# First turn's K and R turned as they come and scaled on the way out of PSUM

## The chip, the cores and the metric

The kernel runs on one core of a Trainium2 chip. A time is the device time of one execution in microseconds (us). Engines are named as in the profile: PE (TensorE matmul), PEld (its weight load), DVE (VectorE), ACT (ScalarE), POOL (GpSimd) and SP (SyncE, which here only issues transfers). A line L353 is a line of the kernel file before the change, unless the text says otherwise.

## The reference, cut to what matters

An RWKV-5 recurrence over 4 batches, 8 heads, 768 steps and head size 48 feeds a router with 8 experts:

```python
for t in range(S):
    cur = einsum('bhd,bhe->bhde', u * k_t, v_t)
    y[:, :, t] = einsum('bhd,bhde->bhe', r_t, state + cur)
    state = w * state + einsum('bhd,bhe->bhde', k_t, v_t)
x = y.transpose(0, 2, 1, 3).reshape(B * S, H * D)      # 3072 rows of 384
logits = normalized(x) @ normalized(expert_emb).T / tau
out[rows of e] = gate * relu(x @ w1[e]) @ w2[e]         # each row to its best expert
```

The change touches only the beginning of the recurrence.

## The kernel before, in words

The 768 steps are cut into 6 chunks of 128, and each chunk is worked in two turns, each with two of the four batches. So there are 12 turns, numbered t = 0 to 11, and the two batches of a turn are called u = 0 and u = 1. Within a chunk the recurrence becomes matrix products: K and R are scaled by powers of the decay w, the scores are R times K transposed under a mask, and a state of 48x48 per head is carried from chunk to chunk.

The steps of a turn, with the functions that issue them:

- `load`: K, R and V come as one transfer of 192 KB each per batch (128 partitions x 8 heads x 48 words); from turn 4 on each is cut in two. Nearly all are issued by SP, in the order of the code; the two of R in turn 0 by ACT's queue.
- `scale_r`, `scale_k` (L353, L348): R and K, rows being steps, times the tables `rpow` and `kpow`. DVE does it in turn 0, POOL in all later turns. For t > 0 the first of a turn waits for the first half of the previous turn's scores.
- `turn_in` (L369): four PE transposes each bring the scaled tile into PSUM. `take_in` (L374, L376): ACT copies the turned tile to SBUF as `KT` and the first half of `RT`. `own_r` (L382): DVE multiplies the turned R by u times w, the second half of `RT`, which serves the step's own term.
- `scores` (L395): 64 PE products per turn. `mask` and `own_terms` (L410, L417): DVE takes them out under the masks `smask` and `dmask`.
- `outer` (L431): scaled K times V, for the state. `half_state`, `next_state` and `decay_state` (L445 to L458) carry the state on DVE and POOL.
- `with_v` (L486) and `with_state` (L505), a turn later, give y; `turn_y` and `take_x` (L520, L524) turn it back into rows, `keep_x` stores them.

Before the first turn `build_first` makes the tables. DVE waits for `w` (four words per partition, two small transfers), fills a step tile, and a scan (L114) makes the powers; L119 and L121 make the tables `kp` (for K) and `rp` (for R) with channels on partitions. PE transposes them (L128) and DVE copies them to `kpow` and `rpow` (L133), with steps on partitions. Ahead of that, PE runs three products of ones (L99, the constant `WAKE`), and a fourth after the tables. POOL makes the identity and the masks.

The order of all other work is written by hand: `attention` puts every step at a planned time (`plan.at`), and the program emits steps in order of those times. The times set only the order in which each engine's instructions stand; each engine runs its own list in order and waits on semaphores. At turn 1 to 3, loads are emitted as K, K, R, R, V, V, three planned periods (9.4 each) ahead. `load_small` fetches the expert embeddings (`emb`), `tau` and w as one row; `embeddings_a` uses `emb` on ACT (L252) and then on POOL (L253 to L258).

SP's list is in order too. Completion of transfers is counted on eight semaphores in rotation, so a transfer waits until the one eight places before it has landed.

```python
def scale_r(k, t, u):
    q = k.nc.gpsimd if t else k.nc.vector
    ins = q.tensor_mul(of(k.Rw, t)[:, u, :, 0:D], of(k.R, t)[:, u], k.rpow)
    if t and u == 0:
        after(k, ins, k.scored)
```

Of the kernel before, what the change touches and what calls it, by code (L numbers as in the profile page):

```python
# [10 lines left out]
F32 = mybir.dt.float32  # L11
# [64 lines left out]
def build_first(k):  # L76

    nc, pool = k.nc, k.const
    wc = k.wc0 = pool.tile([128, NP], F32, name="wc")
    nc.vector.memset(wc, 1.0)  # L80
    k.ones = pool.tile([128, 128], F32, name="ones")
    nc.vector.memset(k.ones, 1.0)
    wide = scratch(k.YT[2], 0)
    nc.vector.memset(wide, 1.0)
    with nc.allow_non_contiguous_dma(reason="384 words"):
        for s in range(2):
            q = nc.sync if s == 0 else nc.scalar
            q.dma_start(out=wc[s * DP : s * DP + D, :], in_=k.w.rearrange("(p s) d -> s d p", s=2)[s])
    for which in range(3):
        for u in range(2):  # L90
            load(k, 0, which, u, paced=False)
    uw = k.aconst.tile([128, NP], F32, name="uw")
    nc.vector.memset(uw, 0.0)
    with nc.allow_non_contiguous_dma(reason="384 words"):
        for s in range(2):
            nc.scalar.dma_start(out=uw[s * DP : s * DP + D, :], in_=k.u.rearrange("(p s) d -> s d p", s=2)[s])

    def idle(i):
        nc.tensor.matmul(k.bank[(6 + i) % 8], k.ones, wide, start=True, stop=True)  # L99

    for i in range(WAKE):
        idle(i)
    k.ident = pool.tile([128, 128], F32, name="ident")
    make_identity(nc, k.ident)
    step, seed = (k.AT[1][:, i].rearrange("q r (p i) -> q (r p) i", i=C) for i in range(2))
    nc.gpsimd.memset(seed, 0.0)
    nc.gpsimd.memset(seed[:, :, 0:1], 1.0)

    nc.vector.tensor_scalar(wc, wc, W_MIN, W_MAX, ALU.max, ALU.min)
# [11 lines left out]
    nc.vector.tensor_mul(rp, t, over_i)  # L121
    k.kpow = k.aconst.tile([128, H, D], F32, name="kpow")
# [7 lines left out]
    build_masks(k)  # L130
    for src, dst, bank in tables:
        ps = bank.rearrange("q (p s d) -> q p s d", p=NP, s=2)
        nc.vector.tensor_copy(dst.rearrange("q (p s) d -> q p s d", s=2), ps[:, :, :, 0:D])  # L133
    k.tables = t, uw


def tables_u(k):
    k.uw = k.aconst.tile([128, NP], F32, name="uw2")
    k.nc.vector.tensor_mul(k.uw, k.tables[1], k.wc0)


def tables_w(k):
# [13 lines left out]
def build_masks(k):  # L156
    nc, pool = k.nc, k.const
    k.umask = pool.tile([128, 128], F32, name="umask")
    nc.gpsimd.memset(k.umask, 0.0)
    nc.gpsimd.affine_select(  # L160
        out=k.umask, in_=k.umask, compare_op=ALU.is_ge, fill=1.0,
        base=0, pattern=[[-1, 128]], channel_multiplier=1,
    )

    k.smask = k.aconst.tile([128, HC], F32, name="smask")
    k.dmask = k.aconst.tile([128, HC], I32, name="dmask")
    for s in range(2):
        nc.vector.tensor_copy(k.smask[halves(s), :], k.umask[halves(s), halves(s)])
        nc.vector.tensor_copy(k.dmask[halves(s), :], k.ident[halves(s), halves(s)])


def numbers(k, name, shape, pattern, base, step):
# [113 lines left out]
def rings(k):  # L286

    nc, pool = k.nc, k.aconst

    def ring(name, count, shape, pad=None, pool=pool):  # L290
        out = []
        for i in range(count):
            t = pool.tile(shape, F32, name=f"{name}{i}")
            if pad is not None:
                nc.gpsimd.memset(t[:, :, :, D:DP], 0.0)
            out.append(t)
        return out

    k.K = ring("K", 3, [128, 2, H, D], pool=k.long)
    k.R = ring("R", 3, [128, 2, H, D], pool=k.long)  # L300
    k.Rw = ring("Rw", 2, [128, 2, H, DP], True, k.long)
    k.V = ring("V", 4, [128, 2, H, DP])
    k.Kw = ring("Kw", 2, [128, 2, H, DP], True, k.long)
# [25 lines left out]
def load(k, t, which, u, part=slice(0, H), paced=True):  # L329

    c, bp = divmod(t, 2)
    src, ring = ((k.k, k.K), (k.r, k.R), (k.v, k.V))[which]
    q = k.nc.scalar if which == 1 and t == 0 else k.nc.sync
    ins = q.dma_start(
        out=of(ring, t)[:, u, part, 0:D],
        in_=src[2 * bp + u, part, c * C : (c + 1) * C, :].rearrange("h s d -> s h d"),
    )
    if paced:
        after(k, ins, k.last)


def pair(t, p):
# [2 lines left out]

def scale_k(k, t, u):
    q = k.nc.gpsimd if t else k.nc.vector
    q.tensor_mul(of(k.Kw, t)[:, u, :, 0:D], of(k.K, t)[:, u], k.kpow)  # L348


def scale_r(k, t, u):
    q = k.nc.gpsimd if t else k.nc.vector
    ins = q.tensor_mul(of(k.Rw, t)[:, u, :, 0:D], of(k.R, t)[:, u], k.rpow)  # L353
    if t and u == 0:
        after(k, ins, k.scored)


# [6 lines left out]


def turn_in(k, t, u, which):
    src, bank = of(k.Kw if which else k.Rw, t), k.turned[u][which]
# [11 lines left out]


def own_r(k, t, u):
    k.nc.vector.tensor_mul(  # L382
        of(k.RT, t)[:, u, :, :, 1, :], k.turned[u][0].rearrange("q (p s i) -> q p s i", p=NP, s=2),
        k.uw[:, :, None, None].to_broadcast([128, NP, 2, HC]),
    )
# [435 lines left out]
def attention(k):  # L821
# [4 lines left out]
    for t in range(TURNS):  # L826
# [3 lines left out]
        for i in range(6 if t else 0):  # L830
            when = at - 3 * P + 0.5 + 1.55 * i
            if t < 4:
                plan.at(when, load, k, t, i // 2, i % 2, slice(0, H), False)
                continue
            for j in range(2):
                plan.at(when + 0.75 * j, load, k, t, i // 2, i % 2, slice(j * NP, (j + 1) * NP))
        for u in range(2):
            for which in range(2):

                place = which if t else 1 - which  # L840
                plan.at(before + 1.0 + 2 * u + place, scale_k if which else scale_r, k, t, u)
                plan.at(before + 3.3 + 2.35 * u + 0.47 * place, turn_in, k, t, u, which)
                plan.at(before + 3.8 + 2.4 * u + 0.6 * place, take_in, k, t, u, which)
            plan.at(before + (4.0 if t else 5.3) + 2.6 * u, own_r, k, t, u)
# [926 lines left out]
```

## Time and profile before

| what | us |
|---|---|
| median of 3 runs (lowest, highest) | 410.56 (407.46, 411.36) |
| the profiled execution, its whole time | 410.78 |
| its span, first to last instruction | 408.9 |
| PE busy in the span | 386.8 (95%) |
| DVE / ACT / POOL busy | 228.0 / 143.6 / 130.2 |
| scores of turns 0, 1, 2, 3 begin | 11.68, 18.23, 27.56, 38.99 |

The profile gives instructions in order of time with start, duration, engine, line, operation, output and inputs, shape and count; in square brackets stands the idle time of the engine before the instruction and what seems to have ended it. DMA figures are means over the core's 16 DMA engines. A start of "SPq" or "ACTq" is the issue of a transfer by that queue, not its data. The trace also records each transfer's packets and the moments at which its semaphore was raised; where the text says that something landed, it is the last of these.

### The profile page before, as it was taken

What the parts mean: (1) busy time and instruction counts of PE and PEld (TensorE: products, weight loads), DVE (VectorE), ACT (ScalarE), POOL (GpSimd) and SP (SyncE); (2) the same over time, 40 slices, a digit from 0 to 9 for tenths busy, and PEclk for the clock granted to TensorE, in tenths of its full rate; (3) what the DMA queues carried; (4) which work ended last, traced back from release to release, by engine and by line L of the source; (5) the groups of instructions that cost most, each with busy time, mean ns of one, the idle gap of its engine ahead of it and who ended that gap; (6) DMA issues with size and microseconds to landing.
All of it is one profiled execution on the core that took longest, in us unless ns stands there. A gap on an engine that the chain in (4) does not pass through costs nothing.

```text
span 408.9 us, 12450 instructions
## 1 busy us (share of the span) xinstructions
PE 386.8 (95%) x5118; PEld 345.3 (84%) x5118; DVE 228.0 (56%) x582; ACT 143.6 (35%) x367; POOL 130.2 (32%) x167
## 2 busy tenths in 40 slices
PE   7888899899998999899999999999999999999993
PEld 3677788797897899879899999999998989979882
DVE  7866677787788580522852645445454464374331
ACT  1355464546462624221133214313412413413400
POOL 2584656564653231602133013104303412012001
PEclk9999999999999999999999999999999999999998
DMA  9998768877717357734834252514605553001001
GB/s 136 159 163 168 150 146 173 171 160 152 155 44 235 117 175 232 247 124 158 299 117 113 101 184 87 159 43 172 194 25 190 142 185 117 0 19 38 2 19 47
DMA packets 95460, 54.40 MB, mean 133 GB/s; under 512 B 78723, under 2 KB 90034, under 8 KB 95394
## 3 DMA queue, kind: packets, MB, share of 16 engines
q1 hardware_dynamic: 89426, 43.67, 42.1%
q0 software_dynamic: 3264, 9.44, 6.9%
q10 hardware_dynamic: 2704, 0.40, 0.7%
q8 instruction: 42, 0.69, 0.7%
q14 instruction: 24, 0.20, 0.2%
HBM read 44.20 MB, written 9.58 MB: 132 GB/s over the span
## 4 chain that ended last, share of the span: by engine, by line
PE 83%; issue 4%; POOL 2%; DVE 1%; ACT 0%; POOLq 0%; DVEq 0%
PE ps L1131 15%; PE ps L1264 12%; PE pu L1131 8%; PE ps L1044 6%; PE pu L1264 5%; PE ps L395 4%; PE ps L1294 4%; PE ps L369 4%; PE ps L1301 3%; PE py L486 3%; PE pu L1294 3%; PE py L1044 2%; PE pu L431 2%; PE pu L520 2%; PE py L505 2%
## 5 line engine op out<-in xcount | busy, mean ns | idle before, releaser
L1233 POOL DMA_INDIRECT out_dram<-y,goes x27 | 30.8, 1140 | 174.0 <-ACT y L1348 90.9
L1011 POOL DMA_INDIRECT G<-xs,take x23 | 24.3, 1058 | 30.6 <-PE py L1031 8.6
L1131 PE MATMUL ps<-xTe,w 128*128 128x192 f32 (+3 forms) x160 | 31.4, 333 | 0.0
L353 POOL TENSOR_TENSOR Rw<-R,rpow 128x384 f32<-128x384 f32 x22 | 22.8, 1034 | 19.4 <-DMA R<-in_r_dram 10.1
L1044 PE MATMUL ps<-RT,w 128*128 128x128 f32 x204 | 26.6, 279 | 1.4 <-ACT K L1047 0.5
L1131 PEld LDWEIGHTS ps<-xTe,w 128*128 128x128 f32 x160 | 27.5, 190 | 0.0
L1286 DVE SCALAR_TENSOR_TENSOR y<-ps,lists_sorted,kept 128x192 f32<-128x192 f32 x18 | 7.1, 416 | 35.6 <-ACT kept L1278 21.8
L1044 PEld LDWEIGHTS ps<-RT,w 128*128 128x128 f32 x204 | 24.3, 192 | 2.4 <-ACT K L1047 1.0
L1264 PE MATMUL ps<-T,RT 128*128 128x192 f32 x144 | 26.0, 328 | 0.0
L395 PE MATMUL ps<-RT,KT 48*64 48x128 f32 x768 | 25.1, 273 | 0.7 <-DVE RT L382 0.5
L395 PEld LDWEIGHTS ps<-RT,KT 48*64 48x64 f32 x768 | 21.3, 133 | 3.9 <-issue 2.9
L1264 PEld LDWEIGHTS ps<-T,RT 128*128 128x128 f32 x144 | 23.6, 190 | 0.6 <-ACT kept L1278 0.6
L348 POOL TENSOR_TENSOR Kw<-K,kpow 128x384 f32<-128x384 f32 x22 | 23.4, 1066 | 0.0
L376 ACT COPY RT<-ps 128x512 f32<-128x512 f32 x24 | 14.1, 588 | 21.0 <-PE ps L369 16.6
L382 DVE TENSOR_TENSOR RT<-ps,uw 128x512 f32<-128x512 f32 x24 | 16.6, 690 | 8.0 <-ACT RT L376 7.9
L1131 PE MATMUL ps<-Tx,S 128*128 128x192 f32 (+3 forms) x96 | 20.3, 341 | 0.0
L1149 ACT COPY kept<-ps 128x384 f32<-128x384 f32 (+3 forms) x24 | 11.8, 490 | 22.7 <-PE ps L1131 17.5
L1061 DVE TENSOR_TENSOR RT<-ps,kept 128x384 f32<-128x384 f32 (+1 forms) x15 | 8.5, 566 | 19.9 <-PE ps L1131 19.5
L410 DVE TENSOR_TENSOR AT<-ps,smask 128x256 f32<-128x256 f32 x48 | 18.5, 412 | 1.4 <-PE ps L395 1.4
L417 DVE COPY_PREDICATED AT<-dmask,ps 128x256 f32<-128x256 int32 x48 | 18.4, 437 | 0.0
L1101 ACT COPY xTe<-py 128x384 f32<-128x384 f32 (+3 forms) x18 | 8.8, 490 | 27.0 <-PE py L1108 26.9
L1131 PEld LDWEIGHTS ps<-Tx,S 128*128 128x128 f32 x96 | 16.1, 190 | 2.1 <-ACT kept L1149 2.1
(342 smaller groups left out, 885.9 us busy)
## 6 DMA issues: line engine op xcount, KB each, us to landing
w<-in_moe_w_dram SPq DMA_DIRECT2D x24, 512.0 KB
w<-in_moe_w_dram SPq DMA_DIRECT2D x32, 384.0 KB
xs<-X SPq DMA_DIRECT2D x24, 192.0 KB
K<-in_k_dram SPq DMA_DIRECT2D x32, 96.0 KB
R<-in_r_dram SPq DMA_DIRECT2D x32, 96.0 KB
V<-in_v_dram SPq DMA_DIRECT2D x32, 96.0 KB
K<-in_k_dram SPq DMA_DIRECT2D x8, 192.0 KB
V<-in_v_dram SPq DMA_DIRECT2D x8, 192.0 KB
```

The source lines that it names most:

```text
L348: q.tensor_mul(of(k.Kw, t)[:, u, :, 0:D], of(k.K, t)[:, u], k.kpow)
L353: ins = q.tensor_mul(of(k.Rw, t)[:, u, :, 0:D], of(k.R, t)[:, u], k.rpow)
L382: k.nc.vector.tensor_mul(of(k.RT, t)[:, u, :, :, 1, :], k.turned[u][0].rearrange("q (p s i) -> q p s i", p=NP, s=2), k.uw[:, :, None, None ...
L395: ins = k.nc.tensor.matmul(k.D[2 * u + par][halves(s), p * C : (p + 1) * C], KT[rows, u, p, halves(s)], RT[rows, u, p, s].rearrange("q j i ...
L410: k.nc.vector.tensor_mul(of(k.AT, t)[:, u, par].rearrange("q (p i) -> q p i", p=NP), kinds(k, u, par)[:, :, 0], k.smask[:, None, :].to_bro ...
L417: k.nc.vector.copy_predicated(of(k.AT, t)[:, u, par].rearrange("q (p i) -> q p i", p=NP), k.dmask[:, None, :].to_broadcast([128, NP, HC]), ...
L1011: k.nc.gpsimd.indirect_dma_start(out=G[0:n, :], out_offset=None, in_=k.xs[0:rows, :], in_offset=IndirectOffsetOnAxis(ap=(k.take_first if f ...
L1044: k.last = k.nc.tensor.matmul(ps, w1[:, m, f * 128 : (f + 1) * 128], x_of(k, e, m)[:, cols], start=(m == 0), stop=(m == NK - 1))
L1131: k.last = nc.tensor.matmul(ps[:, i * h : (i + 1) * h], a[:, g, i * 128 : (i + 1) * 128], b, start=start and i == 0, stop=True, skip_group ...
L1233: k.nc.gpsimd.indirect_dma_start(out=out[:, :], out_offset=IndirectOffsetOnAxis(ap=k.goes[0:n, e, t : t + 1], axis=0), in_=y[0:n, :], in_o ...
L1264: k.last = nc.tensor.matmul(ps, a(q), b[:, q], start=start and q == 0, stop=True, skip_group_check=True,)
L1294: k.last = nc.tensor.matmul(p.z, h_one(k, e, f)[:, 256:384], w2[:, f, :], start=(f == 0), stop=(f == NF - 1))
```

## The change

Five things change, all in the first turns.

- **Turn 0's K and R are turned raw.** They are loaded into `Kw[1]` and `Rw[1]` (the padded tiles that turn 1's scaled K and R will take later), PE turns them unscaled, ahead of the tables' transposes, and DVE multiplies them by `kp` and `rp` (channels on partitions) as it takes them out of PSUM. ACT's four copies of turn 0 and DVE's two scalings of R go. Turn 0's scaled K by rows, which `outer` needs, is made by DVE after that.
- **R times u in turn 0** is done by ACT from SBUF, in four instructions per batch with u times w as a scale column, in place of one DVE instruction from PSUM.
- **Tables and masks.** The tables' transposes and copies move behind the first K and R; ACT makes the copies to `kpow` and `rpow`, and the copies of `smask`. The fourth product of ones goes. POOL's clearing of the pads of `Kw` and `Rw` moves from the start to behind the masks.
- **Order of transfers.** `u` is fetched right behind `w`, ahead of K and R. Then SP's order is: K of turn 0; K, R, K, R of turn 1; V of turn 0; K, R, K, R of turn 2; V of turn 1; V of turn 2; one K of turn 3; `emb`, `tau`, w's row; the other K of turn 3; R and V of turn 3. Before it was K, V of turn 0; K, R, V of turn 1; `emb`, `tau`, w's row; K, R, V of turn 2; K, R, V of turn 3. From turn 4 on it is as before.
- **One wait goes**: the scaling of turn 1's R on POOL no longer waits for turn 0's scores.

```diff
     with nc.allow_non_contiguous_dma(reason="384 words"):
-        for s in range(2):
-            q = nc.sync if s == 0 else nc.scalar
-            q.dma_start(out=wc[s * DP : s * DP + D, :], in_=k.w.rearrange("(p s) d -> s d p", s=2)[s])
-    for which in range(3):
-        for u in range(2):
+        for dst, src in ((wc, k.w), (uw, k.u)):
+            for s in range(2):
+                q = nc.sync if s == 0 else nc.scalar
+                q.dma_start(out=dst[s * DP : s * DP + D, :], in_=src.rearrange("(p s) d -> s d p", s=2)[s])
+
+    for u in range(2):
+        for which in range(2):
             load(k, 0, which, u, paced=False)
...
+    build_masks(k)
+    for X in (k.Kw[1], k.Rw[1], k.Kw[0], k.Rw[0]):
+        nc.gpsimd.memset(X[:, :, :, D:DP], 0.0)
...
+    nc.vector.tensor_mul(k.uw, uw, wc)
+    k.tables = t, rp, kp
+
+
+def tables_rows(k):
+
     k.kpow = k.aconst.tile([128, H, D], F32, name="kpow")
     k.rpow = k.aconst.tile([128, H, D], F32, name="rpow")
-    tables = ((kp, k.kpow, k.U[0]), (rp, k.rpow, k.U[1]))
-    for src, dst, bank in tables:
+    for src, dst, bank in ((k.tables[2], k.kpow, k.U[0]), (k.tables[1], k.rpow, k.U[1])):
         ps = bank.rearrange("q (p s d) -> q p s d", p=NP, s=2)
         for p in range(NP):
-            nc.tensor.transpose(ps[:, p].rearrange("q s d -> q (s d)"), src[:, p, :], k.ident)
-    idle(WAKE)
...
+            k.nc.tensor.transpose(ps[:, p].rearrange("q s d -> q (s d)"), src[:, p, :], k.ident)
+        k.nc.scalar.copy(dst.rearrange("q (p s) d -> q p s d", s=2), ps[:, :, :, 0:D])
...
+    dst = raw(k, which) if t == 0 and which < 2 else of(ring, t)
...
+def raw(k, which):
+    return (k.Kw[1], k.Rw[1])[which]
...
 def scale_k(k, t, u):
     q = k.nc.gpsimd if t else k.nc.vector
-    q.tensor_mul(of(k.Kw, t)[:, u, :, 0:D], of(k.K, t)[:, u], k.kpow)
+    q.tensor_mul(of(k.Kw, t)[:, u, :, 0:D], of(k.K, t)[:, u] if t else raw(k, 0)[:, u, :, 0:D], k.kpow)
 
 
 def scale_r(k, t, u):
-    q = k.nc.gpsimd if t else k.nc.vector
-    ins = q.tensor_mul(of(k.Rw, t)[:, u, :, 0:D], of(k.R, t)[:, u], k.rpow)
-    if t and u == 0:
+    ins = k.nc.gpsimd.tensor_mul(of(k.Rw, t)[:, u, :, 0:D], of(k.R, t)[:, u], k.rpow)
+    if t > 1 and u == 0:
         after(k, ins, k.scored)
...
 def take_in(k, t, u, which):
-    if which:
+    if t == 0:
+        src = k.turned[u][which].rearrange("q (p i) -> q p i", p=NP)
+        if which:
+            k.nc.vector.tensor_mul(of(k.KT, t)[:, u], src, k.tables[2])
+        else:
+            k.nc.vector.tensor_mul(
+                of(k.RT, t)[:, u, :, :, 0, :], src.rearrange("q p (s i) -> q p s i", s=2),
+                k.tables[1].rearrange("q p (s i) -> q p s i", s=2),
+            )
+    elif which:
...
 def own_r(k, t, u):
+    if t == 0:
+        for p in range(NP):
+            R = of(k.RT, t)[:, u, p]
+            k.nc.scalar.mul(R[:, :, 1, :], R[:, :, 0, :], k.uw[:, p : p + 1])
+        return
...
             if t < 4:
-                plan.at(when, load, k, t, i // 2, i % 2, slice(0, H), False)
+
+                if t < 3 and i > 3:
+                    continue
+                plan.at(when, load, k, t, i // 2 if t > 2 else i % 2, i % 2 if t > 2 else i // 2, slice(0, H), False)
+                if t < 3 and i == 3:
+                    for v in ((0,), (1, 2))[t - 1]:
+                        for w in range(2):
+                            plan.at(when + 0.1 * v + 0.01, load, k, v, 2, w, slice(0, H), False)
                 continue
...
-    plan.at(-P + 0.4, load_small, k)
-    plan.at(-P + 5.25, tables_u, k)
+    plan.at(0.6, load_small, k)
+    plan.at(-P + 3.95, tables_rows, k)
+    for u in range(2):
+        plan.at(0.05 + 0.01 * u, scale_k, k, 0, u)
```

More of the change, by code (lines that the diff above doesn't have):

```diff
@@ L80, in build_first @@
     nc.vector.memset(wc, 1.0)
+    uw = k.aconst.tile([128, NP], F32, name="uw")
+    nc.vector.memset(uw, 0.0)
     k.ones = pool.tile([128, 128], F32, name="ones")
@@ L85, in build_first @@
     with nc.allow_non_contiguous_dma(reason="384 words"):
-        for s in range(2):
-            q = nc.sync if s == 0 else nc.scalar
-            q.dma_start(out=wc[s * DP : s * DP + D, :], in_=k.w.rearrange("(p s) d -> s d p", s=2)[s])
-    for which in range(3):
-        for u in range(2):
-            load(k, 0, which, u, paced=False)
[L92 to L96, printed above, removed]
+        for dst, src in ((wc, k.w), (uw, k.u)):
[4 more added lines that the diff above has]
+        for which in range(2):
+            load(k, 0, which, u, paced=False)
     def idle(i):
@@ L121, in build_first @@
     nc.vector.tensor_mul(rp, t, over_i)
+    k.uw = k.aconst.tile([128, NP], F32, name="uw2")
+    nc.vector.tensor_mul(k.uw, uw, wc)
+    k.tables = t, rp, kp
+def tables_rows(k):
     k.kpow = k.aconst.tile([128, H, D], F32, name="kpow")
     k.rpow = k.aconst.tile([128, H, D], F32, name="rpow")
-    tables = ((kp, k.kpow, k.U[0]), (rp, k.rpow, k.U[1]))
-    for src, dst, bank in tables:
+    for src, dst, bank in ((k.tables[2], k.kpow, k.U[0]), (k.tables[1], k.rpow, k.U[1])):
         ps = bank.rearrange("q (p s d) -> q p s d", p=NP, s=2)
         for p in range(NP):
-            nc.tensor.transpose(ps[:, p].rearrange("q s d -> q (s d)"), src[:, p, :], k.ident)
-    idle(WAKE)
[L130 to L139, printed above, removed]
+            k.nc.tensor.transpose(ps[:, p].rearrange("q s d -> q (s d)"), src[:, p, :], k.ident)
+        k.nc.scalar.copy(dst.rearrange("q (p s) d -> q p s d", s=2), ps[:, :, :, 0:D])
 def tables_w(k):
@@ L167, in build_masks @@
     for s in range(2):
-        nc.vector.tensor_copy(k.smask[halves(s), :], k.umask[halves(s), halves(s)])
         nc.vector.tensor_copy(k.dmask[halves(s), :], k.ident[halves(s), halves(s)])
+        nc.scalar.copy(k.smask[halves(s), :], k.umask[halves(s), halves(s)])
 def numbers(k, name, shape, pattern, base, step):
@@ L300, in rings @@
     k.R = ring("R", 3, [128, 2, H, D], pool=k.long)
-    k.Rw = ring("Rw", 2, [128, 2, H, DP], True, k.long)
+    k.Rw = ring("Rw", 2, [128, 2, H, DP], None, k.long)
     k.V = ring("V", 4, [128, 2, H, DP])
-    k.Kw = ring("Kw", 2, [128, 2, H, DP], True, k.long)
+    k.Kw = ring("Kw", 2, [128, 2, H, DP], None, k.long)
     k.RT = ring("RT", 3, [128, 2, NP, 2, 2, HC], pool=k.long)
@@ L333, in load @@
     q = k.nc.scalar if which == 1 and t == 0 else k.nc.sync
+    dst = raw(k, which) if t == 0 and which < 2 else of(ring, t)
     ins = q.dma_start(
-        out=of(ring, t)[:, u, part, 0:D],
+        out=dst[:, u, part, 0:D],
         in_=src[2 * bp + u, part, c * C : (c + 1) * C, :].rearrange("h s d -> s h d"),
@@ L366, in turn_in @@
 def turn_in(k, t, u, which):
-    src, bank = of(k.Kw if which else k.Rw, t), k.turned[u][which]
+    src, bank = of(k.Kw if which else k.Rw, t) if t else raw(k, 1 - which), k.turned[u][which]
     for p in range(NP):
@@ L840, in attention @@
                 place = which if t else 1 - which
-                plan.at(before + 1.0 + 2 * u + place, scale_k if which else scale_r, k, t, u)
+                if t:
+                    plan.at(before + 1.0 + 2 * u + place, scale_k if which else scale_r, k, t, u)
                 plan.at(before + 3.3 + 2.35 * u + 0.47 * place, turn_in, k, t, u, which)
                 plan.at(before + 3.8 + 2.4 * u + 0.6 * place, take_in, k, t, u, which)
-            plan.at(before + (4.0 if t else 5.3) + 2.6 * u, own_r, k, t, u)
+            plan.at(before + (4.0 if t else 4.75) + 2.6 * u, own_r, k, t, u)
             plan.at(at + 0.9 * u, scores, k, t, u)
```

## The prediction, made before the changed kernel was run

> **What bounds the kernel now.** I read the chain that ended last first: PE holds 83% of it, and its traced part begins only at 35.61 us. The change touches turns 0 to 2, that is the first 30 us, so what counts is when each later turn's work may begin on PE, and what that waits for. That is read from the timeline of 0 to 30 us, of every engine:
>
> ```profile
> 3.18 0.29 DVE L109 TENSOR_SCALAR wc<-wc 128x4 f32<-128x4 f32 x1 [1.59 <-DMA wc<-in_w_dram]
> ...
> 7.48 1.02 PE L99 MATMUL ps<-YT,ones 128*128 128x512 f32 x2
> ...
> 11.68 2.08 PE L395 MATMUL ps<-RT,KT 48*64 48x128 f32 x64 [0.48 <-DVE RT L382]
> ...
> 13.52 1.00 POOL L353 TENSOR_TENSOR Rw<-R,rpow 128x384 f32<-128x384 f32 x1 [10.08 <-DMA R<-in_r_dram]
> ...
> 18.23 2.23 PE L395 MATMUL ps<-RT,KT 48*64 48x128 f32 x64
> ...
> 21.06 1.00 POOL L353 TENSOR_TENSOR Rw<-R,rpow 128x384 f32<-128x384 f32 x1 [1.60 <-PE py L486]
> ...
> 27.56 2.09 PE L395 MATMUL ps<-RT,KT 48*64 48x128 f32 x61
> ...
> 29.45 0.20 POOL L258 MEMSET ent<- 128x128 f32 x1
> ...
> 29.62 1.00 POOL L353 TENSOR_TENSOR Rw<-R,rpow 128x384 f32<-128x384 f32 x1
> ```
>
> The scores (L395) of turns 0, 1, 2 begin at 11.68, 18.23, 27.56. Turn 0 hangs on a chain of small steps from `w`. Turns 1 to 3 begin with POOL's scaling of R, and there the trace's landing records (when a transfer's semaphore reached its count) say what releases it: R of turn 1 landed at 13.35 (POOL 13.52), of turn 2 at 20.93 (POOL 21.06, though the view names PE), of turn 3 at 29.39 (POOL 29.62). All three are transfers. The third is the one that matters most below.
>
> The windows of one us, columns PE busy, granted clock, DMA share, GB/s, show that the input stream runs without pause except three times:
>
> ```profile
> 17.00:18.00 1.00, 1.00 (x27) 1.00 1.02 156
> 18.00:19.00 1.00, 1.00 (x31) 1.00 0.11 19
> ...
> 24.00:25.00 1.00, 0.84 (x56) 1.00 0.45 56
> ...
> 28.00:29.00 1.00, 1.00 (x43) 1.00 0.33 67
> ```
>
> Each dip follows, by about 2.3 us, a 16 KB instruction packet (packet records: 16.06, 21.92, 25.95 us, each holding one DMA engine for 1.1 to 1.7 us), while one SP issue takes 2.1 to 2.7 us instead of about 1 (R at 15.61, K at 21.89, V at 26.07). So up to 29 us the loads are a queue of 192 KB pieces, about 1.04 us each, and a piece lands by its place in that queue.
>
> **Part by part: turn 0.** `w` stays first in both queues, so DVE's chain from 3.18 to 6.93 (L109 to L121) stays; the product of u and w adds 0.15, to 7.05. The two mask casts left on DVE (0.19 each) fit its 1.59 idle before 3.18. `u` now stands before K and R: one issue on each queue, 0.40 to 0.42 by the `w` rows, so K and R of the first u land near 5.35 and 5.9 (4.91, 5.44 now), of the second near 7.4 and 8.3 (7.01, 7.83).
> PE ends its third warming matmul at 6.63 (5.20 + 1.43), the fourth (7.48, 1.02) goes. Groups of four transposes start 0.47 apart (9.14, 9.63, 10.10, 10.57 now): K 6.63, R 7.1, the two tables 7.6 and 8.05, K 8.5, R 9.0, end 9.6.
> DVE takes K and R out with the tables, four products of 128x512 for which L382 has 0.69 and L119 to L121 a step of 0.61: 7.3, 7.9, 9.1, 9.75, end 10.45. Gone from DVE are kpow and rpow (0.56, 0.55, now ACT at 8.2 to 9.25), two scalings of R (0.55 each) and two products with u (0.69 each); the two scalings of K (0.55 each) follow at 10.4 to 11.5, with the masks behind them.
> ACT's product with u is four ACTIVATEs for one 0.69. The trace has no such row; bounds are 0.278 each (L1047, 128x128, no scale column) and 0.421 (L1278, 128x192, scale column), 1.1 to 1.7 for four; I take 1.2, since the size is that of the first row. Only the first of the four stands before the scores, and PE waits for each pair's own. First u: 9.2 to 10.4, scores 9.6 to 10.7. Second u: 10.5 to 11.7, scores 10.9 to 12.0. They now end at 13.76: **1.75 earlier**. With 0.42 each it is 1.3, with 0.28 it is 1.85.
> [...]
>
> **Turns 1 and 2.** In queue order R of turn 1 becomes the 6th and 8th of the large pieces (now 9th, 10th), V of turn 0 the 9th and 10th, R of turn 2 the 12th and 14th (now 15th, 16th), V of turn 1 the 15th and 16th (now 11th, 12th). By today's landings of those places: R1 at 10.2 and 12.3, V0 at 13.4 and 14.4, R2 at 16.8 and 20.1, V1 at 20.9 and 22.3, each plus 0.2 (late start) or minus 0.5 (`u`'s 4-byte packets at 7.5 to 8 no longer sit ahead of V0, which took 1.4 a piece).
> So POOL scales turn 1 at 10.4 to 14.4, limited by rpow, R and by DVE's reading of the raw K that it overwrites. Masks of turn 0 end near 14.4 (15.6 now); outer of turn 0 needs V0 at 14.4, so starts near 13.7 and ends 14.8 to 15.3 (17.28 now). Scores of turn 1 start near 16.1 (2.1 earlier). R of turn 2 is scaled after the scores' first half and `decay_state`, near 18.0 (21.06 now); V1 at 22.3 holds outer of turn 1 to an end near 22.6 (25.7 now). Scores of turn 2 start near 24.6, some **3.0 earlier**, and PE is through with turn 1's products at about 27.7 (30.67 now).
>
> **Turn 3 takes most of it back.** R of turn 3 is the 21st large piece before and after; V1 and V2 are ahead of it as before, so nothing got shorter. Its data went from 26.31 to 27.35, its landing was late (29.39) because the packet at 25.95 held one engine. That packet follows PE's progress, so it comes near 23 instead: the third dip (0.75) then falls ahead of the piece and the late engine does not. 27.35 + 0.75, 0.2 more or 0.5 less, gives 27.6 to 28.3; with some lateness left, up to 29.4. Emb, tau and w's row now sit between the two K pieces of turn 3, their three issues 1.0 + 0.29 + 0.25. POOL's queue has `embeddings_a` ahead of Rw of turn 3; from ACT L252 (27.32) to POOL 29.62 that is 2.3, so a landing of emb at 25.2 to 26.0 (K of turn 3 landed at 25.2) gives 27.5 to 28.3. I take 28.4 for POOL's start: 29.62 - 28.4 = **1.2 earlier**. From there PE's order is the same and dense (R turned 30.67, scores 38.99), so 1.2 stays. Turn 4's R landed at 38.29 and POOL took it at 40.24: slack 1.95, enough for 1.2.
>
> Smaller edits cost nothing: pad memsets behind the masks on POOL end near 3.9, before K and R land; smask on ACT follows the table load (1.28) in its idle until 8.2.
>
> **The sum.** The profiled execution took 410.78 (span 408.9, 1.9 around it); less 1.2 is 409.6. It stands 0.2 above the median of the runs shown, 410.56, on whose scale the forecast is 409.4. The runs spread from 407.46 to 411.36, so about 1% is what a measurement can tell from no change.
>
> **Rivals.** (1) *The gain is carried whole.* If R of turn 3 lands before 27, POOL waits for the scores of turn 2 alone and up to 3.0 stays: 407.6. For it: no dip need recur. Against: three dips in 29 us. (2) *Slower: emb's landing.* In POOL's queue Rw of turn 3 stands 2.3 behind it. It decides from a landing of 27.3 (29.62 - 2.3). If the three small issues meet a blocked ring and the stream starves for their 1.5, emb and R land near 28.2 and 30.4: POOL at 30.5, 0.9 late, 411.5. Against: SP runs two to three pieces ahead. (3) *Turns 1 to 3 stay where they are*, V0 (moved behind four pieces) being caught by the packet that comes as outer starts: one engine late by 1.7, V0 at 16.1, outer ends at 16.9, 0.4 early; and R of turn 3 at 29.4. Then 410.3.
>
> **How the numbers follow.** Forecast (0.8 to 1.8 kept) 0.5; rival 1 0.2; rival 2 0.15; rival 3 0.15. The range takes in rivals 1 and 2 with the spread of a median: 407.2 to 411.5. Faster by over 1% (below 406.45) needs more than rival 1: 0.1. Slower by over 1% (above 414.67): 0.06. Within: 0.84.
>
> **What would show it.** Right: scores of turn 0 near 9.6, of turn 1 near 16, of turn 2 near 24.6, then PE idle until turn 3's R is turned near 29.5 (30.67 now), POOL's wait there ending on R or on emb; scores of turn 3 near 37.8 (38.99). Wrong: outer of turn 0 waiting for V past 15, an ACT wait of over 2 on emb, or turn 3 not at all earlier while turn 2 is.

## The result, and the profile after

| | median of 22 runs, us | lowest to highest | profiled execution: time, span |
|---|---|---|---|
| before | 409.77 | 407.46 to 412.49 | 410.78, 408.9 |
| after | 409.14 | 406.80 to 412.24 | 407.85, 406.0 |

The ratio is 0.9973, with a 95% interval of 0.995 to 0.9997. It is that of the means (408.91 to 410.00); the medians give 0.9985. Either way it is less than 1%, and 409.14 lies inside the forecast (409.4, range 407.2 to 411.5). The profiled executions differ by 2.9 us, far more than the medians, so one profile against one profile says little about the total here.

The timeline of 0 to 30 us of the kernel after (start, duration, engine, line, operation, output and inputs, shape, count, and in brackets the idle time ahead and its end). `scores` is now L411, `own_r` L396, `scale_r` L355, `outer` L447:

```profile
9.34 2.54 ACT L396 ACTIVATE RT<-RT,uw 128x128 f32<-128x128 f32 x8
...
9.79 2.58 PE L411 MATMUL ps<-RT,KT 48*64 48x128 f32 x64
...
10.99 1.37 POOL L355 TENSOR_TENSOR Rw<-R,rpow 128x384 f32<-128x384 f32 x1 [7.54 <-ACT RT L396]
...
14.26 0.68 PE L447 MATMUL pu<-V,Kw 64*64 64x48 f32 x32 [0.22 <-DMA V<-in_v_dram]
...
15.40 0.68 PE L447 MATMUL pu<-V,Kw 64*64 64x48 f32 x32 [0.46 <-DMA V<-in_v_dram]
...
17.04 2.23 PE L411 MATMUL ps<-RT,KT 48*64 48x128 f32 x64
...
22.24 1.78 PE L447 MATMUL pu<-V,Kw 64*64 64x48 f32 x64 [0.41 <-DMA V<-in_v_dram]
...
25.91 1.98 PE L411 MATMUL ps<-RT,KT 48*64 48x128 f32 x64
...
26.89 0.52 ACT L250 ACTIVATE X<-X 8x384 f32<-8x384 f32 x1 [1.17 <-DMA X<-in_moe_expert_emb_dram]
...
29.02 0.19 POOL L256 MEMSET ent<- 128x128 f32 x1
...
29.34 0.99 POOL L355 TENSOR_TENSOR Rw<-R,rpow 128x384 f32<-128x384 f32 x1
```

Turn 0 starts its scores 1.89 earlier (11.68 before), turn 1 1.19 (18.23), turn 2 1.65 (27.56). But POOL scales turn 3's R at 29.34, against 29.62: 0.28 earlier. Of the head start of turn 2 little is left there. PE shows where it goes (the timeline of 26 to 52 us, same columns), the kernel after:

```profile
30.38 0.65 PE L371 MATMUL ps<-ident,Rw 128*128 128x128 f32 x4 [1.58 <-POOL Rw L355]
...
37.57 1.98 PE L411 MATMUL ps<-RT,KT 48*64 48x128 f32 x64
```

The kernel before:

```profile
30.67 0.66 PE L369 MATMUL ps<-ident,Rw 128*128 128x128 f32 x4
...
33.93 1.03 PE L431 MATMUL pu<-V,Kw 64*64 64x48 f32 x56 [0.92 <-issue]
...
38.99 1.98 PE L395 MATMUL ps<-RT,KT 48*64 48x128 f32 x64
```

After the change PE stands idle for 1.58 until that R is scaled, an idle time that the kernel before does not have (its R was turned at 30.67 with no wait shown). The windows of one us (length, busy time of PE, PEld, DVE, ACT and POOL with instruction counts, granted clock, DMA share, GB/s) show that idle time and the dips of the input stream:

```profile
17.00:18.00 1.00, 1.00 (x33) 0.86 (x32) 1.00 (x2) 0.78 (x2) 0.58 (x1) 1.00 0.50 71
...
25.00:26.00 1.00, 1.00 (x13) 0.75 (x15) 1.00 (x3) 0.72 (x2) 0.64 (x1) 1.00 0.27 45
...
29.00:30.00 1.00, 0.00 (x0) 0.00 (x0) 0.83 (x3) 0.51 (x4) 0.88 (x3) 1.00 1.08 173
```

The dips at 17 and 25 again follow 16 KB instruction packets (15.1, 19.9 and 23.7 us in the packet records; 16.1, 21.9 and 25.9 before); behind the one at 19.9 the rate fell only to 118 GB/s, at 22. In this profile the packets came 0.9 to 2.3 earlier, with the work, but the dips did not go.

Turn 3's scores do start 1.42 earlier (38.99 before). Most of that is a wait that the first profile of before has and this one lacks (PE's 0.92 in `outer` of turn 2, at 33.93, "issue": it ends on nothing that the profile shows). Repeated profiles below show that it is not a property of the kernel: from the turning of that R to the scores it is 8.32 in the first profile of before and 7.18 to 7.53 in the thirteen others.

### The profile page after: what moved, and what is told of

Its sections match the earlier page's. It is cut to its first block, busy times and chain, and to the rows that moved or that the text cites. A ratio compares the mean times of both kernels' runs of the same rounds, so it can differ in the third digit from the quotient of the medians.

```text
span 406.0 us, 12451 instructions
## 1 busy us (share of the span) xinstructions
PE 385.4 (95%) x5116; PEld 346.1 (85%) x5116; DVE 227.0 (56%) x578; ACT 146.0 (36%) x375; POOL 130.6 (32%) x167
## 4 chain that ended last, share of the span: by engine, by line
PE 82%; DMA 4%; issue 3%; DVE 1%; POOL 0%; POOLq 0%; SPq 0%
PE ps L1157 15%; PE ps L1290 12%; PE pu L1157 8%; PE ps L1070 5%; PE pu L1290 5%; PE ps L371 4%; PE ps L1320 4%; PE ps L411 4%; PE ps L1327 3%; PE pu L536 3%; PE pu L1320 3%; PE py L502 2%; PE py L1070 2%; PE py L1134 2%; PE pu L447 2%
## 5 line engine op out<-in xcount | busy, mean ns | idle before, releaser
L355 POOL TENSOR_TENSOR Rw<-R,rpow 128x384 f32<-128x384 f32 x22 | 23.1, 1051 | 16.6 <-PE ps L411 8.4
L411 PE MATMUL ps<-RT,KT 48*64 48x128 f32 x768 | 25.0, 274 | 0.3 <-issue 0.2
L411 PEld LDWEIGHTS ps<-RT,KT 48*64 48x64 f32 x768 | 21.0, 133 | 3.7 <-issue 2.7
L387 ACT COPY RT<-ps 128x512 f32<-128x512 f32 x22 | 12.9, 586 | 19.9 <-PE ps L371 17.9
L1087 DVE TENSOR_TENSOR RT<-ps,kept 128x384 f32<-128x384 f32 (+1 forms) x15 | 8.5, 566 | 19.9 <-PE ps L1157 19.9
L398 DVE TENSOR_TENSOR RT<-ps,uw 128x512 f32<-128x512 f32 x22 | 15.2, 689 | 6.8 <-ACT RT L387 6.7
L371 PE MATMUL ps<-ident,Rw 128*128 128x128 f32 x96 | 15.4, 282 | 3.6 <-POOL Rw L355 1.6
```

Of the source, the lines that this page charges most:

```text
L355: ins = k.nc.gpsimd.tensor_mul(of(k.Rw, t)[:, u, :, 0:D], of(k.R, t)[:, u], k.rpow)
L411: ins = k.nc.tensor.matmul(k.D[2 * u + par][halves(s), p * C : (p + 1) * C], KT[rows, u, p, halves(s)], RT[rows, u, p, s].rearrange("q j i ...
```

## Experiments

All kernels compute the whole reference. They ran in three groups, each on one chip and each beside 35 runs of the kernel before there (medians 410.01, 410.80, 410.23). "POOL R3" is the start of POOL's scaling of turn 3's R, "scores" the start of turn 0 to 3 on PE.

### Group 1: what holds turn 3

The first theory was that turn 3 is held by the landing of R and by the work on `emb` ahead of it on POOL. Each was moved forward alone, then both, then POOL's own list as well.

**R of turn 3 ahead** of V of turn 2 (edit of after):

```diff
-                if t < 3 and i > 3:
+                if i > 3:
                     continue
-                plan.at(when, load, k, t, i // 2 if t > 2 else i % 2, i % 2 if t > 2 else i // 2, slice(0, H), False)
-                if t < 3 and i == 3:
-                    for v in ((0,), (1, 2))[t - 1]:
+                plan.at(when, load, k, t, i % 2, i // 2, slice(0, H), False)
+                if i == 3:
+                    for v in ((0,), (1,), (2, 3))[t - 1]:
```

> The changed kernel with K and R of turn 3 fetched ahead of V of turn 2 (R's first piece from 21st to 18th place); emb, tau and w's row still right behind turn 3's first K. Theory (turn 3 is held by two things that end together, R's landing at 29.20 and POOL's work on emb, ending 29.21): R lands near 25.5, but emb now lands near 24.5 at best, POOL's work on it ends near 27.5 to 28.5, so POOL scales turn 3's R at 27.5 to 28.5 (29.34 in the changed kernel), 0.8 to 1.8 earlier, and PE's idle 1.58 before its transposes shrinks to 0 to 0.8. Rival (R's landing alone held it): POOL starts at 27.0, as soon as turn 2's scores allow, PE idle 0. Rival (the hold is harmless, later waits absorb it): scores of turn 3 not earlier than 37.6. Total: theory 0.2% to 0.4% under the changed kernel, last rival 0.

**`emb` fetched early**, between V of turn 0 and K of turn 2 (edit of after):

```diff
-    plan.at(0.6, load_small, k)
+    plan.at(-P + 0.4, load_small, k)
```

> The changed kernel with emb, tau and w's row fetched where the kernel before had them, between V of turn 0 and K of turn 2; the rest of the order as in the changed kernel. Theory: ACT's wait of 1.17 for emb goes and POOL's work on emb ends near 28.0 instead of 29.21, but R of turn 3 still lands near 29.2, so POOL scales it at 29.3, PE idles about 1.5 as before, no gain (0 to 0.1%). Rival (emb held turn 3): POOL starts at 28.0 to 28.2, 1.2 earlier, about 0.3% gained.

**Both**:

> Both: emb between V of turn 0 and K of turn 2, and K and R of turn 3 ahead of V of turn 2. Theory: R lands near 25.6, emb near 15.5; POOL's work on emb runs after ACT's square at 25.8 and ends near 28.0, and turn 3's R is scaled right behind it, 28.0 to 28.2; R's transposes near 29.1 instead of 30.38, PE idle 0.3 instead of 1.58, scores of turn 3 1.2 earlier than 37.57. Total 0.3% under the changed kernel. Rival (later waits absorb it): the same early picture, but the total equals the changed kernel's within 0.1%, turn 4 or 5 starting no earlier.

**Both, and POOL's work on `emb` a turn earlier** (on top of both; the tile `half` is filled ahead):

```diff
-    plan.at(P + 6.9, embeddings_a, k)
+    plan.at(5.0, embeddings_a, k)
```

> As the last, and the work on emb on ACT and POOL moved into turn 1, where POOL idles 1.16 before the state's decay. Theory: nothing but turn 2's scores holds the scaling of turn 3's R, which starts near 27.0; R's transposes follow turn 1's last products without idle time near 28.8, scores of turn 3 1.5 to 1.6 earlier than the changed kernel's 37.57; total 0.35% to 0.4% under the changed kernel, about 0.65% under the kernel before. Rival (later waits absorb it): early picture the same, total as the changed kernel.

| | median, us | ratio to before (95%) | POOL R3 | PE idle ahead of R3 | scores of turn 3 |
|---|---|---|---|---|---|
| R ahead | 407.72 | 0.9963 (0.9931 to 0.9995) | 27.94 | 0.15 | 36.18 |
| `emb` early | 409.22 | 0.9983 (0.9949 to 1.0018) | 28.64 | 0.86 | 36.88 |
| both | 407.99 | 0.9961 (0.9922 to 1.0000) | 28.73 | 0.27 | 36.96 |
| both, and POOL | 408.86 | 0.9970 (0.9939 to 1.0001) | 27.69 | none | 36.55 |

The timelines tell what POOL waited for. With R ahead:

```profile
27.77 0.19 POOL L256 MEMSET ent<- 128x128 f32 x1
...
27.94 1.00 POOL L355 TENSOR_TENSOR Rw<-R,rpow 128x384 f32<-128x384 f32 x1
...
28.99 0.66 PE L371 MATMUL ps<-ident,Rw 128*128 128x128 f32 x4 [0.15 <-POOL Rw L355]
```

With `emb` early:

```profile
27.77 0.19 POOL L256 MEMSET ent<- 128x128 f32 x1
...
28.64 1.00 POOL L355 TENSOR_TENSOR Rw<-R,rpow 128x384 f32<-128x384 f32 x1 [0.68 <-DMA R<-in_r_dram]
...
29.70 0.66 PE L371 MATMUL ps<-ident,Rw 128*128 128x128 f32 x4 [0.86 <-POOL Rw L355]
```

With both, and POOL's list changed:

```profile
27.69 1.01 POOL L355 TENSOR_TENSOR Rw<-R,rpow 128x384 f32<-128x384 f32 x1 [0.98 <-PE ps L411]
...
29.27 0.66 PE L371 MATMUL ps<-ident,Rw 128*128 128x128 f32 x4
```

In the first the R tile is in (landed at 24.63) and POOL starts right behind its `emb` work (27.77 + 0.19); in the second that work is done at the same moment and POOL waits 0.68 for R (landed at 28.50); in the third it waits for turn 2's scores alone and PE has no wait. So both holds are real. In the first profile of the changed kernel they end together (`emb` work at 29.21, R landed at 29.20), and with either one out of the way the other still holds. With R ahead the `emb` work is also early, since `emb`'s own last packet then landed at 22.93 instead of 26.87. With both, POOL's start is again right behind the `emb` work, whose last row came late because turn 2 did (scores at 26.61 for 25.91):

```profile
28.56 0.20 POOL L256 MEMSET ent<- 128x128 f32 x1
...
28.73 0.99 POOL L355 TENSOR_TENSOR Rw<-R,rpow 128x384 f32<-128x384 f32 x1
```

Three of the four expectations missed POOL's start by 0.4 to 0.7: with `emb` early R came earlier too, so POOL began at 28.64, which neither side foresaw (29.3 or 28.0 to 28.2); with both it was 28.73 for 28.0 to 28.2; with POOL's list changed 27.69 for 27.0. The totals do not follow the starts: the kernel with no hold left does not have the lowest median, and given their intervals the four are not apart.

### Group 2: the parts alone, and both kernels again

**Only the new order of transfers** (edit of before; turn 0's arithmetic stays):

```diff
-        for s in range(2):
-            q = nc.sync if s == 0 else nc.scalar
-            q.dma_start(out=wc[s * DP : s * DP + D, :], in_=k.w.rearrange("(p s) d -> s d p", s=2)[s])
-    for which in range(3):
-        for u in range(2):
-            load(k, 0, which, u, paced=False)
...
+        for dst, src in ((wc, k.w), (uw, k.u)):
...
+    for u in range(2):
+        for which in range(2):
+            load(k, 0, which, u, paced=False)
...
-                plan.at(when, load, k, t, i // 2, i % 2, slice(0, H), False)
+                if t < 3 and i > 3:
+                    continue
+                plan.at(when, load, k, t, i // 2 if t > 2 else i % 2, i % 2 if t > 2 else i // 2, slice(0, H), False)
+                if t < 3 and i == 3:
+                    for v in ((0,), (1, 2))[t - 1]:
...
-    plan.at(-P + 0.4, load_small, k)
+    plan.at(0.6, load_small, k)
```

> The kernel before with the changed order of transfers alone (u behind w, K and R of turns 1 and 2 ahead of V, emb and its two neighbours behind turn 3's first K); turn 0 still scales first and turns then, u by DVE. Theory (the transfers set turns 1 to 3, the way turn 0 is computed sets only turn 0): scores of turn 0 at 11.7 to 12.2, turn 1 at 17.0 to 18.0 (18.23 before, 17.04 changed), turn 2 at 25.5 to 26.5 (27.56, 25.91), POOL's scaling of turn 3's R at 29.2 to 29.6 as in both, total like the changed kernel's within 0.1%: 0.2 to 0.3% under the kernel before. Rival (turning K and R raw is what gains): turns 1 and 2 at their times of before, total as before.

**Only turn 0's arithmetic** (after, with the transfers in the order of before: the same lines the other way round, `u` behind K, R and V again):

> The changed kernel with the order of transfers of the kernel before (u behind R on ACT's queue, V of each turn with its turn, emb between turns 1 and 2); K and R of turn 0 still turned raw, u by ACT. Theory: scores of turn 0 at 9.3 to 10.5, then R of turn 1 lands near 13.4 as before, scores of turn 1 at 17.8 to 18.3, turn 2 at 27.3 to 27.6 behind R at 20.9, turn 3's R scaled at 29.3 to 29.7: the 1.9 of turn 0 is lost at the first transfer, total as the kernel before within 0.1%. u may come late: it lands at 9.5 and stands ahead of DVE's first product, then turn 0 starts at 11.5. Rival (raw turning is what gains): turns 1 and 2 as early as in the changed kernel, 0.27% gained.

**The kernel before, unchanged, as one of the kernels under test**:

> The kernel before once more, for a second profile and its granted clocks. Theory: what differs between two executions of one kernel is the clock granted in the experts' part (the changed kernel's runs: 0.978 to 0.992, 407 to 412, some 3 per 0.01) and where PE waits for its instructions; the first 30 us repeat within 0.5: turns 0 to 3 begin at 11.7, 18.2, 27.6 and 38 to 39, turn 3's R is scaled at 29.3 to 30. Median of the clock 0.986 to 0.990 as for the changed kernel. Rival (the earlier attention part lowers the clock): 0.993 or more here, and so a real gain of 2.5 shows as 1.1.

**The kernel after, unchanged**:

> The changed kernel once more, for a second profile. Theory: turns 0 to 2 begin at 9.8, 17.0, 25.9 within 0.5, turn 3's R is scaled at 28.5 to 29.5 with PE idle 0.8 to 1.6 before its transposes, turn 3 at 37 to 38. Ratio to the kernel before 0.995 to 0.9995.

| | median, us | ratio to before (95%) | scores of turns 0, 1, 2, 3 | POOL R3 |
|---|---|---|---|---|
| order alone | 410.32 | 1.0002 (0.9972 to 1.0033) | 11.67, 17.63, 26.27, 36.70 | 28.45 |
| turn 0 alone | 410.70 | 1.0007 (0.9975 to 1.0039) | 11.93, 18.70, 27.41, 37.83 | 29.53 |
| before again | 409.26 | 0.9969 (0.9935 to 1.0003) | 11.68, 18.41, 27.16, 37.77 | 29.21 |
| after again | 409.17 | 0.9961 (0.9929 to 0.9993) | 9.92, 17.02, 26.41, 37.76 | 29.18 |

The row to read first is the third. The kernel before, compared with itself, comes out at 0.9969, as far off as the change. And its second profile has turn 3's scores at 37.77 where the first had 38.99: at most 0.2 later than the changed kernel's 37.57 and 37.76. The timeline of this second profile of before:

```profile
29.04 0.20 POOL L258 MEMSET ent<- 128x128 f32 x1
...
29.21 1.00 POOL L353 TENSOR_TENSOR Rw<-R,rpow 128x384 f32<-128x384 f32 x1
...
30.27 0.66 PE L369 MATMUL ps<-ident,Rw 128*128 128x128 f32 x4
...
37.77 1.98 PE L395 MATMUL ps<-RT,KT 48*64 48x128 f32 x64
```

That R is turned at 30.67 and 30.27 in the two profiles of before, at 30.38, 30.23 and 30.45 in three of after. At turn 3 the change has gained 0.1 on average, less than two profiles of one kernel differ by.

The rival of this run's expectation, that the change lowers the clock, asked for a clock of 0.993 or more here, and the median was 0.9955. But the 35 runs of the kernel before beside it had 0.992 and the changed kernel 0.993, so the change lowered no clock.

The order alone gives the contrary picture, here its timeline:

```profile
28.45 1.00 POOL L352 TENSOR_TENSOR Rw<-R,rpow 128x384 f32<-128x384 f32 x1
...
29.51 0.66 PE L368 MATMUL ps<-ident,Rw 128*128 128x128 f32 x4 [0.34 <-POOL Rw L352]
...
36.70 1.98 PE L394 MATMUL ps<-RT,KT 48*64 48x128 f32 x64
```

Turn 3 starts 1.07 ahead of the second profile of before, and the total is the same as before; both the start of POOL (28.45 for 29.2 to 29.6) and the total went against the expectation. By turn 11 the lead is gone in this profile (scores at 118.59, against 117.79). So a lead at turn 3 is not a lead at the end.

With turn 0's arithmetic alone `u` is again behind the large pieces (its second half landed at 10.05). DVE's small product of u and w waits for it, and stands ahead of DVE's products out of PSUM (line number of that kernel):

```profile
10.07 0.16 DVE L126 TENSOR_TENSOR uw<-uw,wc 128x4 f32<-128x4 f32 x1 [3.12 <-DMA uw<-in_u_dram]
```

So the scores start at 11.93, no earlier than before: as this half of the change is written, it needs the other one. What it would give with that product further back in DVE's list was not run.

### Group 3: the fourth product, and repeats

The next theory was that what counts is where an instruction stands in PE's list against the borders of its 16 KB packets, since the change takes instructions out ahead of them.

**Before without the fourth product of ones**:

```diff
-    idle(WAKE)
     build_masks(k)
```

> The kernel before without the fourth product of ones, nothing else: PE's list is four instructions shorter, as the changed kernel's is, and where PE crosses from one 16 KB block of its instructions to the next moves by four. Theory (place in the list): the waits of PE that end on nothing shown, which differ between the kernels with the fourth product (5.2, 3.2, 4.4 from 27 to 122 us) and one without it (3.1 with the old order), follow the place: turns 0 to 3 begin as in the kernel before, and these waits are 3 to 4; 1.0 to 1.5 faster at equal granted clock. Rival (chance, and what gains is turning raw): turns 0 to 3 as before, no difference at equal clock (under 0.7).

**After with one small further product** (its result is not used):

```diff
     for i in range(WAKE):
         idle(i)
+    nc.tensor.matmul(k.bank[(6 + WAKE) % 8][:, 0:8], k.ones, wide[:, 0:8], start=True, stop=True)
```

> The changed kernel with a fourth product of ones, 8 columns wide, behind the three: four PE instructions more, under 0.3 us on PE. Theory (place in the list): the changed kernel's gain of about 1 at equal clock goes, and the waits of PE that end on nothing shown move to other lines. Rival: as the changed kernel within 0.7, the waits on the same lines (L371, L447).

**Turn 0's arithmetic alone, and the kernel after, once more**:

> The changed kernel with the old order of transfers once more. Theory (turn 3 is held in either order, so the order is worth nothing alone): within 0.7 of the changed kernel at equal clock, turn 3's R scaled at 29.2 to 29.7. Rival (the new order costs): 0.5 or more faster than the changed kernel again, with 2 less of PE's unexplained waits between 27 and 122 us.

> The changed kernel for a third profile: turn 3's R scaled at 28.5 to 29.5, turn 3 at 37 to 38; at equal clock 0.4 to 1.6 faster than the kernel before.

| | median, us | ratio to before (95%) | scores of turns 0, 1, 2, 3 |
|---|---|---|---|
| before without the fourth | 409.82 | 0.9990 (0.9961 to 1.0019) | 12.05, 18.11, 26.89, 37.35 |
| after with a small further one | 410.47 | 1.0011 (0.9981 to 1.0041) | 9.47, 17.02, 25.92, 38.09 |
| turn 0 alone again | 409.59 | 0.9991 (0.9966 to 1.0016) | 11.77, 18.66, 28.09, 38.78 |
| after, third time | 408.50 | 0.9984 (0.9953 to 1.0015) | 9.43, 17.11, 26.30, 37.64 |

As measured the first two lean the way the theory wants (taking out helps, putting in hurts), but neither is apart from the kernel before, and the difference shrinks when the clock is taken out (next part). What the theory said of PE's unexplained waits, those of 27 to 122 us that end on nothing shown, did not come. Without the fourth product they add up to 5.4, for 3 to 4 expected. With the further product they are 4.9 and stand on the same steps as in the changed kernel, as the rival had it. And turn 0's arithmetic alone, whose 3.1 the theory had built on, has 4.6 in its second profile, with POOL's start at turn 3 at 30.20 for 29.2 to 29.7. So the runs give the theory no support; an effect on the total below some 0.7 they cannot exclude.

With the small further product `emb` was complete only at 27.55, and POOL scaled turn 3's R at 29.87, later than in either profile of before.

### All runs together

The run times of one kernel go with the granted clock of each run. A straight-line fit to all 271 runs that have a clock on record (a constant for each group of runs and each kernel, one slope for the clock) gives -2.8 ± 0.3 us for +0.01 of clock and leaves a scatter of 1.06 us in place of 1.6. By such fits, without and with the clock, against the kernel before, in us with 95% intervals (the first comparison has no clocks for its runs of before, so it counts in the first column only):

| | as measured | at equal clock |
|---|---|---|
| after | -1.1 ± 0.6 (46 runs) | -1.0 ± 0.5 (24 of them) |
| R of turn 3 ahead | -2.1 ± 1.0 | -2.1 ± 0.7 |
| `emb` early | -1.1 ± 1.0 | -1.5 ± 0.7 |
| both | -1.7 ± 1.0 | -2.0 ± 0.7 |
| both, and POOL | -1.4 ± 1.0 | -1.7 ± 0.7 |
| order alone | 0.0 ± 1.0 | +0.5 ± 0.7 |
| turn 0 alone | 0.0 ± 0.7 | -1.4 ± 0.5 |
| before without the fourth | -0.5 ± 1.0 | -0.4 ± 0.7 |
| after with a further product | +0.7 ± 1.0 | -0.5 ± 0.7 |

Within the second group the kernel before had a median clock of 0.992 in its 35 runs and 0.9955 in the 12 runs of the kernel before as a test; that makes 1.0 of the 1.5 us between them, and at equal clock they differ by -0.2 ± 0.7. So most of the 0.9969 of that comparison went with the clock.

The change itself is worth about 1 us by either column. Fetching R of turn 3 ahead has the lowest median of all versions run: 407.72, at equal clock 1.1 ± 0.9 below the change. It is the best of several picked afterwards, and it was run in one group only.

## Why the prediction was right, and where it was not

**The total: right, but not by its route.** Forecast 1.2 us less; measured 0.6 between the medians of the first comparison, 1.1 between its means, 1.0 to 1.1 over all runs; "within 1%" held the largest chance. The 1.2 was to be won at POOL's start of turn 3 and kept from there. Neither happened, so that the two numbers are alike is luck as far as the runs show. Of the three signs of being wrong that the prediction named, one came (`outer` of turn 0 waits for V until 15.40, past 15), one came nearly (POOL at turn 3 is 0.28 earlier while turn 2 is 1.65 earlier), and one did not (ACT's wait on `emb` is 1.17, not over 2).

**Turn 0: right.** Scores at 9.79, 9.92 and 9.43 in three profiles, forecast 9.6. ACT's four products of a batch took 1.27 (eight in 2.54), forecast 1.2 between bounds of 1.1 and 1.7. The third product of ones ended at 7.05, 7.15 and 6.50, for 6.63 taken, and DVE's first product out of PSUM began at 7.53, 7.65 and 6.98, forecast 7.3. Dropping the fourth product cost nothing that shows: four transposes of turn 0's R take 0.60 in the second profile of after (0.63 in the second of before). Nor did idle time ahead of later transposes slow them in these traces: those at 13.59 take 0.63 behind 1.08 in the second profile of after, those at 14.58 take 0.66 behind 0.81 in the first of before, where the first four of turn 0, at 9.14, take 0.66 too.

**The queue ahead of turns 1 and 2: the mechanism right, one term mis-sized.** The term is the 0.40 to 0.42 for `u` ahead of K and R, and with it the "plus 0.2 (late start) or minus 0.5" of the later landings. `u` was priced at one issue on each queue, with K and R near 5.35 and 5.9. They landed at 5.81 and 6.39, against 4.91 and 5.44 in the first profile of before: 0.9 later, not 0.45 (the second profile of before has 5.11 and 5.64, so 0.7). The single-part runs bear it out: K landed at 5.72 with the new order alone (`u` first), and at 5.06 and 5.02 with turn 0's arithmetic alone (`u` behind). The rest of the stream kept that: the first R of turn 1 landed at 10.86 for 10.2 forecast, V of turn 0 at 14.22 and 15.36 for 13.4 and 14.4. V of turn 1 came at 22.20 and 23.30 for 20.9 and 22.3, and there one late increment adds its part: fifteen of sixteen increments were in by 21.10 and 22.27. `outer` waits for both V in the profile above. So turn 1 began at 17.04 for 16.1, and turn 2 at 25.91 for 24.6.

**Turn 3: the right two holds, at the wrong time.** This is the step that failed, though the total was right. POOL's start was put at 28.4 and came at 29.34, 29.18 and 29.40 in three profiles, 29.62 and 29.21 before. Two terms were off, and both for the same reason: they took the end of the data for the landing. A transfer counts as landed when the last of its semaphore increments is raised. R was worked out from 27.35, where its data ended before. Its data did end within the forecast 27.6 to 28.3 (near 27.8, counting SP's 192-byte packets in the order of their starts). But the first of its sixteen increments came at 27.88, the fifteenth at 28.74 and the last at 29.20 (before: 27.31, 28.03, 29.39); "some lateness left" was allowed for and not taken.

`emb` was put at 25.2 to 26.0 because "K of turn 3 landed at 25.2". That is the fifteenth increment of this K in the first profile of before, too; its last came at 26.35. `emb` was complete at 26.87, 25.88 and 27.08: eight of its nine increments by 25.42 to 25.69, the last up to 1.45 after them. Rival 2's outcome, a late `emb` that holds POOL, so came within 0.5 of its point of decision (27.3) in two of three profiles, by one late increment and not by a starved stream.

Two more readings of the kernel before bear on this: POOL's start at 29.62 stood right behind its `emb` work there (29.45 + 0.20), not behind R alone, and `emb` itself had landed at 17.14. So moving `emb` back made its landing a hold that it had not been.

In the end "PE idle until R is turned" came true (1.58 in the first profile, 0.93 and 1.26 in the others), and "1.2 stays" did not: at turn 3, though not at turns 1 and 2, rival 3's picture holds, a start where it was.

**From turn 3 on: "the same and dense, so 1.2 stays" is refuted as a reason.** The time from turn 3's scores to turn 11's was 82.03 and 80.02 in two profiles of the same kernel before, 80.93, 81.45 and 80.38 in three of the kernel after, and 79.60 to 81.89 in the rest. A spread of 2.4 lies in these turns. The first profile of before, from which the prediction was read, was a long execution: 410.78 at a clock of 0.996, where the second took 407.30 at 0.994. PE's waits that end on nothing the profile shows make up much of the difference. The view of PE's waits from 27 to 122 us (what was waited for: us in all, times, longest), first profile of before:

```profile
PE pu L431 <- issue: 3.1, 4, 0.9
...
PE py L505 <- issue: 1.2, 3, 0.7
PE ps L369 <- issue: 0.7, 1, 0.7
```

second profile of before:

```profile
PE pu L431 <- issue: 1.3, 2, 0.8
PE py L505 <- issue: 1.0, 2, 0.6
PE ps L369 <- issue: 0.9, 1, 0.9
```

profile of after:

```profile
PE ps L371 <- issue: 2.5, 3, 1.3
PE ps L371 <- POOL Rw L355: 1.6, 1, 1.6
PE pu L447 <- issue: 1.3, 1, 1.3
PE py L521 <- issue: 0.7, 1, 0.7
```

The rows "issue" add up to 5.0, 3.2 and 4.5 (5.2, 3.2 and 4.7 with the smaller ones). They vary more between two executions of one kernel than between the two kernels. So does the time from turn 11's scores to the end: 287.9 and 287.6 before, 287.5, 288.6 and 287.4 after. The order alone led by 1.07 at turn 3 and gained nothing; R ahead led by 1.6 over the second profile of before and gained 2.1 ± 0.7.

**What stays open** is where the measured 1 us of the change is gained. It is not at the turning of turn 3's R, where the profiles are alike; behind it one profile against another cannot tell, since two of the kernel before lie 1.2 apart at turn 3's scores and 3.2 at turn 11's. As measured, neither half alone gains and both together do; at equal clock the half with turn 0's arithmetic gains 1.4 without starting any turn earlier, and the order nothing. The two readings contradict each other, and the runs made do not settle it: turn 0's arithmetic alone had clocks of 0.985 in both its groups, beside 0.992 and 0.987 of the kernel before, and whether a kernel lowers its own clock was not shown. The packet-border theory is no way out, since its two runs did not show the waits that it foretold.

## What to carry to other kernels

Follow a head start to the first resource that did not move: here the queue of loads and POOL's list gave back at turn 3 what three turns had won, and two holds that ended together (within 0.5 in three profiles) meant that removing one showed only part. Count a transfer as landed at its last semaphore increment, not where its data or most of its engines are through: for `emb` here the two were up to 1.45 apart. Price a small transfer put ahead of a stream by what it does to the stream's first landing (0.7 to 0.9 us here), not by its issue (0.4). Before explaining a difference below 1%, run the old kernel against itself and look at the clock: that alone was 0.3% here.

## What the runs showed of the hardware

- In the fit over all runs a granted clock higher by 0.01 goes with 2.8 us less of 409, at 95% PE busy; the median clocks of 12 and of 35 runs of one kernel in one group still differed by 0.0035, which is 1.0 us or 0.24%, so here medians of unlike clock are not comparable below that.
- A small transfer can finish late by one straggler: eight of `emb`'s nine increments were in by 25.42, the ninth at 26.87; in the second profile of the same kernel the ninth came 0.20 after the eighth. A 16 KB instruction packet had started at 23.7 in the first; that it held that engine is inferred from the times, not shown by a run.
- The 16 KB instruction packets recur every 4 to 6 us from 15 us on, and in the first profile of each kernel the input stream's dips (19, 56 and 67 GB/s before; 45 and 71, against 140 to 221 in the slices beside them, after) follow them by some 2 us. That the packets cause the dips is inferred from the times; no run changed the packets alone, and behind the packet at 19.9 there was no such dip.
